# Loading w_in in row halves, two-half products for blocks 4 to 11, a cast of v on GpSimd and one more early product

## The chip, the cores and the metric

The kernel runs on one core of one Trainium2 chip. The core has a matrix engine (TensorE, PE in the profile; its weight loads are PEld), VectorE (DVE), ScalarE (ACT), GpSimd (POOL), a queue engine (SyncE, SP) and 16 DMA engines that all queues share. The metric is the device time of one execution in microseconds; of several runs the median is used.

## The reference, cut to what matters

Linear attention for 8 batches of 8 heads, 576 tokens and 64 columns, and on its output, as 4608 tokens of 512 columns, a two-layer network with a "snake" activation:

```
q_s = softmax of q over the 64 columns;  k_s = softmax of k over the 576 tokens
kv  = k_s^T v            (64 x 64 per batch and head)
x   = q_s kv             (4608 x 512, heads side by side)
h   = x @ w_in           (512 -> 2048)
g   = h + sin(alpha * h)^2 / alpha
out = g @ w_out          (2048 -> 512)
```

All inputs and the output are f32; the kernel computes its products in bf16 with f32 accumulation.

## The kernel before, in words

**Tiles.** The 4608 tokens make nine tiles of 512. For a tile, `mm_h` makes h in 16 blocks of 128 hidden columns: each block is four products (one per 128 rows of w_in, called chunks, taken in the order `KO` = 0, 2, 1, 3) of 128 x 128 weights on 512 tokens, accumulated in one PSUM bank. `sine` then runs the sine on ACT and the square on ACT, GpSimd or DVE (a letter string tells which: A, P, D), and `combine` adds h and the scaled square on DVE into `g`. `mm_o` and the generators `o_quad` and `o_stream` make the output from g and w_out.

**Order.** Everything is issued in the order in which the program is written (a manual schedule): each engine works through its own instructions in that order and waits on semaphores. Nothing is reordered.

**The start.** SP loads halves of batch 0's q, k and v. GpSimd waits for the first half of k (`held`, L355), then issues from its own queue the second half of v in two pieces (columns j 0 to 4, and 5 to 8) and all of w_in, converting f32 to bf16 on the way (`load_win`, L108): columns 0 to 255 and 256 to 511 of chunks 0 and 2; columns 0 to 511 of chunks 1 and 3; four transfers of 256 columns with all four chunks (columns 512 to 1535); columns 1536 to 2047; then the first half of w_out in two transfers (L111). All but the 512 KB ones of the last columns and of w_out carry 128 or 256 KB as they arrive in bf16. ACT makes the exponentials, DVE the sums and the normalization of q; two casts bring the second half of v to bf16 (`cast_v0`, L352), both on DVE. `wide_mm` makes kv, `attn_x` makes x, which goes to `xT` by ACT and DVE. x comes in two halves: chunks 0 and 2 of tile 0 first, chunks 1 and 3 later.

**Early products.** Between the first half of x and the second, three products of tile 0 are issued (block 0, chunks 0 and 2; block 1, chunk 0). After the products that make the second half of x, five more follow (block 1 chunk 2, blocks 2 and 3 with chunks 0 and 2). Then the main loop of tile 0 goes through the 16 blocks: blocks 0 to 3 get their chunks 1 and 3, blocks 4 to 15 all four in one go (`h_slot`, with `flush(lag, 1)`, so that the combine lags one block behind).

**Banks.** `BANKS[0]` gives tile 0's blocks their PSUM banks: blocks 0, 1 the two of kind a; 2, 3 b; 4 k (a single bank that also holds kv); 5, 6 l; 7, 8 a; 9, 10 b; 11 k; 12, 13 l; 14, 15 a. A bank is free for its next user when the combine of its block has read it: block 7 waits for block 0's, block 8 for 1's, 11 for 4's, 12 for 5's. The first four outputs of tile 0 take b, b, l, l, so the third waits for block 12's combine.

**What hangs on the loop.** After blocks 6 and 12 a tiny DVE copy (`load_q1`, L464) releases the SP queue to load batch 1: the first half of q behind the first copy, the second half of q and all of k and v behind the second. After blocks 8 and 10 GpSimd issues the next parts of w_out (rows of blocks 8 to 11, then 12 and 13), behind the squares that stand ahead on it. Batch 1's attention (L498 casts its v) runs between tile 0's output products; its x gives tile 1.

Of the kernel before, what the change touches and what calls it, by code (L numbers as in the profile page):

```python
# [23 lines left out]
def kernel(  # L24
# [82 lines left out]
    def load_win(c0, c1, cc=slice(0, 4)):  # L107
        nc.gpsimd.dma_start(out=win[:, cc, c0:c1], in_=win_v[:, cc, c0:c1])  # L108
# [159 lines left out]
    def bank(kind):  # L268

        if kind == "k":  # L270
            return ps_k.tile([128, 2, MF], F32, name="kvp", tag="a")[:, 0]
        pool = {"a": lambda: ps_h[0], "b": lambda: ps_h[1], "l": lambda: ps_l, "o": lambda: ps_o[0], "p": lambda: ps_o[1]}[kind]()
        return pool.tile([128, MF], F32, name={"l": "lp", "o": "op", "p": "op"}.get(kind, "hp"), tag=kind)

    def mm_h(t, ni, k0=0, k1=4):

        if ni == 0 and k0 == 0:
            G[t] = gpool.tile([128, nN, MF], BF16, name="g")
        hp = HP[t, ni] if k0 else bank(BANKS.get(t, 3 * "aabb" + "abba")[ni])
        HP[t, ni] = hp  # L280
        for k in range(k0, k1):
            nc.tensor.matmul(hp, win[:, KO[k], ni * 128:(ni + 1) * 128],  # L282
                             xT[:, KO[k], t * MF % NX:t * MF % NX + MF], start=(k == 0), stop=(k == 3))
        return hp

    def sine(t, ni, hp, sq):
        s = spool.tile([128, MF], F32, name="s")
        nc.scalar.activation(s, hp, AX.Sin, scale=alpha_sb[:, ni:ni + 1])  # L288
        if sq == "A":
            nc.scalar.activation(s, s, AX.Square)  # L290
        elif sq == "P":
            nc.gpsimd.tensor_tensor(s, s, s, op=ALU.mult)  # L292
        else:
            nc.vector.tensor_tensor(s, s, s, op=ALU.mult)
        return s
# [25 lines left out]
    ACT_CP, DVE_CP, GP_CP = nc.scalar.copy, nc.vector.tensor_copy, nc.gpsimd.tensor_copy  # L321
# [28 lines left out]
    def cast_v0(ii, j0, j1, eng):  # L350
        vv = vb[0].rearrange("p j (i c) -> p i j c", i=4)
        eng(vv[:, 2 * ii:2 * ii + 2, j0:j1, 0:D], staged["v", 0][:, ii::2, j0:j1])  # L352
# [5 lines left out]
    for c in range(2):  # L358
        load_win(256 * c, 256 * c + 256, slice(0, 4, 2))
    load_win(0, 512, slice(1, 4, 2))  # L360
    for c in range(2, 6):
        load_win(256 * c, 256 * c + 256)
    load_win(1536, 2048)
    for c in range(2):
        load_wout(4 * c, 4 * c + 4)
# [41 lines left out]
    tp1 = ps_l.tile([128, 8, 128], BF16, name="tp", tag="l")  # L407
    q_transpose_ii(0, 1, 0, 8, tp1)
    ACT_CP(alpha_sb, tpa)
    cast_v0(1, 0, 5, DVE_CP)  # L410
    cast_v0(1, 5, 9, DVE_CP)
    DVE_CP(A["qT", 0][:, 1, 0:8], tp1)

# [4 lines left out]
    wide_mm(0, 1)  # L418
    wide_norm(0, 1)
    nc.vector.reciprocal(inva_sb, alpha_sb)  # L420
    for ni, ki in ((0, 0), (1, 0), (0, 1)):
        mm_h(0, ni, ki, ki + 1)
    xp = [bank("l") for _ in range(2)]
    attn_x(0, 1, 0, 8, xp)
    for x in range(2):
        (ACT_CP, DVE_CP)[x](xT[:, 2 * x + 1, 0:MF], xp[x])
    nc.scalar.activation(zero, zero, AX.Sin)
    for ni, ki in ((1, 1), (2, 0), (2, 1), (3, 0), (3, 1)):
        mm_h(0, ni, ki, ki + 1)

    def h_slot(t, ni, sq, lag):
        hp = mm_h(t, ni, 2 if ni < (4, 2, 0)[min(t, 2)] else 0)
        lag.append((t, ni, hp, sine(t, ni, hp, sq)))

    def flush(lag, keep):
        while len(lag) > keep:
            combine(*lag.pop(0))
# [21 lines left out]
    with ES:  # L459
        def load_q1(ii):  # L460
            if ii == 0:
                staged["q", 1] = stage.tile([128, 4, J, D], F32, name="st_q", tag="st")
            st = staged["q", 1]
            DVE_CP(st[:, ii, 0, 0:1], zero)  # L464
            nc.sync.dma_start(out=st[:, ii::2, 0:8].rearrange("p i j d -> p i (j d)"),
                              in_=src_view(q, 1)[:, ii::2, 0:8 * D])

        def load_kv1():
            for n in "kv":
                staged[n, 1] = stage.tile([128, 4, J, D], F32, name=f"st_{n}", tag="st")  # L470
            for n, t, ii, j0, j1 in (("k", k, 0, 0, J), ("v", v, 0, 0, J), ("k", k, 1, 0, J),
                                     ("v", v, 1, 0, 5), ("v", v, 1, 5, J)):
                nc.sync.dma_start(out=staged[n, 1][:, ii::2, j0:j1].rearrange("p i j d -> p i (j d)"),
                                  in_=src_view(t, 1)[:, ii::2, j0 * D:j1 * D])

        late = {6: lambda: load_q1(0), 8: lambda: load_wout(8, 12), 10: lambda: load_wout(12, 14),
                12: lambda: (load_q1(1), load_kv1())}
        for ni in range(nN):
            h_slot(0, ni, "DPPAPPAPPAAPPAPD"[ni], lag)
            flush(lag, 1)  # L480
            if ni in late:
                late[ni]()
# [95 lines left out]
        for ni in range(nN):  # L578
            h_slot(1, ni, SQ[ni], lag)
            flush(lag, 1)  # L580
            if ni == 6:
                scale_q8()
            late_q8(ni)
# [69 lines left out]
    for ni in range(nN):  # L653
        h_slot(2, ni, SQ2[ni], lag)
        flush(lag, 2)
        if ni == 5:
            attn_kv(3)
        elif ni in (9, 13):
            ii = ni // 12
            x_copy(DVE_CP, slice(ii, 4, 2), 3, x_pair(3, ii))  # L660
    flush(lag, 0)

    for t in range(3, nT):
# [11 lines left out]
        for ni in range(nN):  # L675
            hp = mm_h(t, ni)
# [62 lines left out]
```

## Time and profile before

| what | value |
|---|---|
| time, median of 3 runs | 282.33 us (281.98 to 282.49) |
| profiled execution | 283.14 us, span in the profile 281.3 us |
| TensorE busy | 268.4 us, 95% |
| ACT / DVE / GpSimd busy | 224.2 / 187.1 / 80.2 us |
| granted TensorE clock | 0.999 |
| DMA | 46.06 MB, mean 164 GB/s |

The span is the time from the first to the last instruction in the profile of one execution; the execution's own time is a little longer. The timeline rows are: start in us, duration in us, engine, line, operation, output <- inputs, shape, number of merged instructions, and in brackets the idle time before with what ended it. In rows of stretches (start:end) the columns are the length, the busy time of PE, PEld, DVE, ACT and POOL with their counts, the granted clock, the DMA engines' share and GB/s.

### The profile page before, as it was taken

To read this page: it belongs to the slowest core of one execution; us is meant where nothing else is said; L and a number is where in the kernel's file an instruction comes from. 1 tells how busy PE (TensorE), PEld (TensorE's weight loads), DVE (VectorE), ACT (ScalarE), POOL (GpSimd) and SP (SyncE) were. 2 spreads that over 40 slices of the span, in tenths; PEclk is the share of its full clock that TensorE was granted. 3 is DMA by queue.
4 is the path that set the end of the run, shared out by engine and by line. 5 is a ranking of instruction groups with operands and counts; after the bars stand their busy time and mean duration, and the time that the engine had idled before them with its cause. 6 is when DMAs were issued, how large, how long until landed. Compare 5 with 4: busy or idle time off the path is not lost.

```text
span 281.3 us, 4775 instructions
## 1 busy us (share of the span) xinstructions
PE 268.4 (95%) x1814; PEld 124.2 (44%) x1843; DVE 187.1 (67%) x279; ACT 224.2 (80%) x321; POOL 80.2 (28%) x75
## 2 busy tenths in 40 slices
PE   3899999999999999999999999999999999999994
PEld 1434454444444444444444444444444444444443
DVE  2968867999878767766776677577775555555422
ACT  4799457999588999899989998999877777777400
POOL 2959112678667450215011500350000000000000
PEclk9999999999999999999999999999999999999999
DMA  7999999795699039811981199125011111111143
GB/s 258 299 185 224 276 385 401 266 356 198 156 245 379 3 76 294 336 37 43 328 332 37 40 267 384 37 51 123 10 30 37 37 40 37 38 42 44 41 100 75
DMA packets 39607, 46.06 MB, mean 164 GB/s; under 512 B 17040, under 2 KB 22944, under 8 KB 39584
## 3 DMA queue, kind: packets, MB, share of 16 engines
q1 hardware_dynamic: 33952, 41.11, 46.1%
q0 software_dynamic: 5472, 4.52, 9.8%
q8 instruction: 14, 0.23, 0.3%
q10 hardware_dynamic: 160, 0.13, 0.2%
q14 instruction: 9, 0.07, 0.1%
HBM read 36.71 MB, written 9.44 MB: 164 GB/s over the span
## 4 chain that ended last, share of the span: by engine, by line
PE 87%; DMA 8%; POOL 2%; issue 1%; ACT 0%; SPq 0%; DVE 0%
PE hp L282 38%; PE op L302 37%; DMA wout<-in_moe_w_out_dram 4%; PE hp L302 2%; DMA win<-in_moe_w_in_dram 2%; PE lp L282 2%; DMA st_k<-in_k_dram 2%; PE kvp L173 2%; PE lp L302 1%; PE op L282 1%; PE op L709 1%; PE hp L237 1%; POOL s L292 1%; PE xp L237 1%; PE kvp L282 1%
## 5 line engine op out<-in xcount | busy, mean ns | idle before, releaser
L298 DVE SCALAR_TENSOR_TENSOR g<-s,inva_sb,hp 128x512 bf16<-128x512 f32 x129 | 95.1, 745 | 58.9 <-ACT s L290 53.3
L282 PE MATMUL hp<-xT,win 128*128 128x512 bf16 x508 | 128.8, 379 | 0.8 <-DMA win<-in_moe_w_in_dram 0.4
L302 PE MATMUL op<-wout,g 128*128 128x512 bf16 x463 | 117.6, 379 | 1.7 <-issue 1.3
L288 ACT ACTIVATE s<-hp,alpha_sb 128x512 f32<-128x512 f32 x129 | 87.0, 684 | 21.8 <-PE hp L282 20.3
L282 PEld LDWEIGHTS <-win 128*128 128x128 bf16 x576 | 55.6, 98 | 68.4 <-DMA win<-in_moe_w_in_dram 1.8
L302 PEld LDWEIGHTS <-g 128*128 128x128 bf16 x560 | 53.4, 98 | 65.4 <-issue 2.9
L290 ACT ACTIVATE s<-s 128x512 f32<-128x512 f32 x112 | 70.7, 632 | 3.6
L292 POOL TENSOR_TENSOR s<-s 128x512 f32<-128x512 f32 x28 | 29.5, 1066 | 17.8 <-ACT s L288 17.7
L152 POOL TENSOR_TENSOR qn<-qe,qs 128x1152 bf16<-128x1152 bf16 x11 | 23.2, 2128 | 30.7 <-DVE qs L146 26.3
L314 DVE COPY o<-op 128x512 f32<-128x512 f32 (+2 forms) x32 | 21.1, 660 | 9.7 <-PE op L302 7.4
L137 POOL CAST vb<-st_v 128x1152 bf16<-128x1152 f32 x12 | 14.4, 1228 | 44.5 <-DMA st_v<-in_v_dram 44.2
L118 ACT ACTIVATE qe<-st_q 128x1152 bf16<-128x1152 f32 (+2 forms) x18 | 17.7, 1026 | 6.3 <-DMA st_q<-in_q_dram 6.1
L118 ACT ACTIVATE ke<-st_k 128x1152 bf16<-128x1152 f32 x16 | 17.9, 1153 | 2.6 <-DMA st_k<-in_k_dram 2.6
L145 DVE TENSOR_REDUCE qs<-qe 128x36 f32<-128x2304 bf16 x5 | 12.8, 2552 | 8.3 <-ACT qe L118 8.3
L302 PE MATMUL hp<-wout,g 128*128 128x512 bf16 x45 | 12.0, 379 | 0.5 <-DMA wout<-in_moe_w_out_dram 0.3
L118 ACT ACT_TABLE_LOAD x7 | 9.0, 1283 | 0.8 <-PEq L723 0.7
L302 PE MATMUL lp<-wout,g 128*128 128x512 bf16 x32 | 9.2, 379 | 0.1
L369 PE MATMUL warm<-st_q,ident 128*128 128x512 f32 (+1 forms) x6 | 4.1, 806 | 4.7 <-DMA st_q<-in_q_dram 4.7
L282 PE MATMUL lp<-xT,win 128*128 128x512 bf16 x32 | 7.7, 379 | 0.4 <-DMA win<-in_moe_w_in_dram 0.4
L250 DVE CAST xT<-xp 128x1024 bf16<-128x1024 f32 (+1 forms) x7 | 7.4, 1065 | 0.0
L298 DVE SCALAR_TENSOR_TENSOR g<-s,inva_sb,lp 128x512 bf16<-128x512 f32 x8 | 5.7, 739 | 0.4 <-POOL s L292 0.4
L108 POOL DMA_DIRECT2D win<-in_moe_w_in_dram x8 | 5.9, 772 | 0.0
(98 smaller groups left out, 137.2 us busy)
## 6 DMA issues: line engine op xcount, KB each, us to landing
out_dram<-o SPq DMA_DIRECT2D x70, 128.0 KB, 2.3
st_q<-in_q_dram SPq DMA_DIRECT2D x6, 1152.0 KB, 6.3
st_k<-in_k_dram SPq DMA_DIRECT2D x6, 1152.0 KB, 9.1
st_v<-in_v_dram SPq DMA_DIRECT2D x6, 1152.0 KB, 11.3
st_k<-in_k_dram SPq DMA_DIRECT2D x4, 576.0 KB, 8.3
st_q<-in_q_dram SPq DMA_DIRECT2D x4, 512.0 KB, 6.2
wout<-in_moe_w_out_dram POOLq DMA_DIRECT2D x3, 512.0 KB, 13.7
win<-in_moe_w_in_dram POOLq DMA_DIRECT2D x5, 256.0 KB, 7.9
```

The lines of the kernel that those rows point to most:

```text
L118: nc.scalar.activation(dst[:, :, ii * 128:(ii + 1) * 128].rearrange("p j (x d) -> p x j d", x=2), src[:, ii::2], AX.Exp)
L137: engs[ii](vv[:, 2 * ii:2 * ii + 2, :, 0:D], staged["v", b][:, ii::2])
L145: nc.vector.tensor_reduce(qs, A["qe", b].rearrange("p j (i d) -> p j i d", i=4), axis=AXL.X, op=ALU.add)
L152: engs[ii % len(engs)].tensor_tensor(qn[:, ii, 0:j1].rearrange("p j (x d) -> p j x d", x=2), qe[:, ii], part.unsqueeze(3).to_broadcast([12 ...
L250: eng(xT[:, c, d0:d0 + m - n], xp[..., n:m])
L282: nc.tensor.matmul(hp, win[:, KO[k], ni * 128:(ni + 1) * 128], xT[:, KO[k], t * MF % NX:t * MF % NX + MF], start=(k == 0), stop=(k == 3))
L288: nc.scalar.activation(s, hp, AX.Sin, scale=alpha_sb[:, ni:ni + 1])
L290: nc.scalar.activation(s, s, AX.Square)
L292: nc.gpsimd.tensor_tensor(s, s, s, op=ALU.mult)
L298: nc.vector.scalar_tensor_tensor(G[t][:, ni], in0=s, scalar=inva_sb[:, ni:ni + 1], in1=hp, op0=ALU.mult, op1=ALU.add)
L302: nc.tensor.matmul(acc, G[t][:, ni, j * 128:(j + 1) * 128], wout[:, ni, :], start=(ni == 0), stop=(ni == nN - 1))
L314: eng(o[:, cols], acc)
```

## The change

- Columns 512 to 1535 of w_in come in four transfers as before, but each has 512 columns and two chunks: columns 512 to 1023 with chunks 0 and 2, then with chunks 1 and 3; then columns 1024 to 1535 likewise.
- The first of the two casts of v's second half (j 0 to 4) moves from DVE to GpSimd, where it stands between the first and the second of these transfers.
- Four instead of three early products are issued ahead of the second half of x (block 1, chunk 2 in addition), and so four instead of five behind it.
- Blocks 4 to 11 of tile 0 are made in two halves: before block 4, the chunk 0 and 2 products of blocks 4, 5, 6 and 7; before block 8, those of 8 to 11; the loop then adds chunks 1 and 3, block by block.

One cast changes its engine; otherwise no instruction is added or taken away, and the number of DMAs and their bytes stay.

```diff
-    for c in range(2, 6):
-        load_win(256 * c, 256 * c + 256)
+    load_win(512, 1024, slice(0, 4, 2))
+    cast_v0(1, 0, 5, GP_CP)
+    load_win(512, 1024, slice(1, 4, 2))
+    for r in range(2):
+        load_win(1024, 1536, slice(r, 4, 2))
     load_win(1536, 2048)
...
     ACT_CP(alpha_sb, tpa)
-    cast_v0(1, 0, 5, DVE_CP)
     cast_v0(1, 5, 9, DVE_CP)
     DVE_CP(A["qT", 0][:, 1, 0:8], tp1)
...
-    for ni, ki in ((0, 0), (1, 0), (0, 1)):
+    for ni, ki in ((0, 0), (1, 0), (0, 1), (1, 1)):
         mm_h(0, ni, ki, ki + 1)
...
-    for ni, ki in ((1, 1), (2, 0), (2, 1), (3, 0), (3, 1)):
+    for ni, ki in ((2, 0), (2, 1), (3, 0), (3, 1)):
         mm_h(0, ni, ki, ki + 1)
...
-        hp = mm_h(t, ni, 2 if ni < (4, 2, 0)[min(t, 2)] else 0)
+        hp = mm_h(t, ni, 2 if ni < (12, 2, 0)[min(t, 2)] else 0)
...
         for ni in range(nN):
+            for n in range(ni, ni + 4) if ni in (4, 8) else ():
+                mm_h(0, n, 0, 2)
             h_slot(0, ni, "DPPAPPAPPAAPPAPD"[ni], lag)
```

## The prediction

> **What bounds the kernel now.** I read the page first (busy shares and slices), then the chain that ended last, then only the stretch that the edit touches: TensorE's timeline from 10 to 46 us with what ended its idle time, the ACT, DVE and GpSimd timelines beside it, the stretches with their DMA rates, and the queue's own waits.
>
> ```profile
> PE 268.4 (95%) x1814; PEld 124.2 (44%) x1843; DVE 187.1 (67%) x279; ACT 224.2 (80%) x321; POOL 80.2 (28%) x75
> DMA  7999999795699039811981199125011111111143
> ```
>
> TensorE is busy 95% of the span, and the 16 DMA engines are full in the first eight slices (to about 56 us). TensorE's instructions stay the same in number and kind, so the time can change only by TensorE's idle time. After 60 us it shows nothing but gaps of 0.16 us that no wait explains; what can be won or lost lies before 45 us.
>
> ```profile
> 12.83 0.82 PE L282 MATMUL hp<-xT,win 128*128 128x512 bf16 x2
> 13.62 0.41 PE L237 MATMUL lp<-qT,kvw 64*64 64x512 bf16 x4
> 15.57 1.90 PE L282 MATMUL hp<-xT,win 128*128 128x512 bf16 x8 [0.36 <-DMA win<-in_moe_w_in_dram]
> 17.31 1.03 PE L282 MATMUL kvp<-xT,win 128*128 128x512 bf16 x4
> 19.90 3.62 PE L282 MATMUL hp<-xT,win 128*128 128x512 bf16 x16
> 23.36 0.81 PE L282 MATMUL kvp<-xT,win 128*128 128x512 bf16 x3
> 24.55 1.90 PE L282 MATMUL lp<-xT,win 128*128 128x512 bf16 x8 [0.39 <-DMA win<-in_moe_w_in_dram]
> 29.74 1.89 PE L302 MATMUL lp<-wout,g 128*128 128x512 bf16 x8
> 35.39 0.38 PE L302 MATMUL hp<-wout,g 128*128 128x512 bf16 x1 [0.30 <-DMA wout<-in_moe_w_out_dram]
> ```
>
> These are tile 0's products. Sixteen take 3.46 us (19.90 to 23.36), so one starts every 0.216 us and ends 0.38 us after its start. There are three waits, each for a transfer: before 15.57 (the third w_in transfer), before 24.55 (columns 1536 to 2047) and before 35.39 (w_out 8 to 11). A gap is counted from the last product's end, so the issue time lost is different: the product after 23.36's four could start at 24.22, so 0.33 is lost there; 32 products after 28.02 end their issue at 34.93, so 0.46 is lost at the third.
>
> ```profile
> 9.20 6.33 DMA win<-in_moe_w_in_dram
> 24.54 10.81 DMA wout<-in_moe_w_out_dram
> 17.20:21.20 4.00, 4.00 (x21) 1.80 (x20) 3.48 (x6) 3.95 (x7) 3.22 (x4) 1.00 1.40 203
> 21.20:24.50 3.30, 2.96 (x14) 1.27 (x13) 2.86 (x5) 3.24 (x7) 2.81 (x3) 1.00 1.23 204
> ```
>
> The chain gives the landings: 15.53 and 35.35, after 6.3 and 10.8 us in the queue. The two stretches (last column GB/s) are the same queue with 256-column rows (17.2 to 21.2) and with 512-column rows (21.2 to 24.5): 203 and 204 GB/s.
>
> ```profile
> 16.28 2.42 ACT L288 ACTIVATE s<-hp,alpha_sb 128x512 f32<-128x512 f32 x4
> 19.27 0.67 ACT L288 ACTIVATE s<-kvp,alpha_sb 128x512 f32<-128x512 f32 x1
> 20.02 2.04 POOL L292 TENSOR_TENSOR s<-s 128x512 f32<-128x512 f32 x2 [0.35 <-ACT s L288]
> 21.10 0.75 DVE L298 SCALAR_TENSOR_TENSOR g<-s,inva_sb,kvp 128x512 bf16<-128x512 f32 x1
> 28.28 1.41 DVE L298 SCALAR_TENSOR_TENSOR g<-s,inva_sb,lp 128x512 bf16<-128x512 f32 x2 [0.19 <-POOL s L292]
> SPq L465 <- DVE st_q L464: 23.9, 2, 19.1
> ```
>
> ACT works without a break from 16.28 to 29.1, half a microsecond behind TensorE. Sine, square and combine of block 4 free bank k at 21.85; the combine of block 12 frees the first lp bank at 29.03, and its second user wants it at 29.74. The last line is the SP queue, which stands behind a tiny DVE copy before it may load batch 1.
>
> **The change part by part.** The sum is made on the profiled execution (span 281.3, 283.14 with what lies around it, 0.81 above the median of 282.33), and its difference is put on the median.
>
> *GpSimd's cast.* GpSimd's 640-element cast takes 0.73 us (at 41.77) where DVE took 0.48. The piece of v that it reads lands 4.8 us after its issue at 6.14, at 10.98; the fourth w_in issue is over at 10.65. So the cast runs from 11.0 to 11.75 and the six transfers queued behind it on GpSimd (three row halves of w_in, columns 1536 on, w_out twice) are issued 1.1 us later. What covers it: these landed 7.9 to 16.7 us after their issue, against 4.8 for the first ones, so they wait for DMA engines, not for GpSimd; and GpSimd stood idle 2.48 us before its first square at 17.63. Cover gone, it costs up to 1.1. DVE gains nothing: its other cast waits for the second piece (issued 7.04, 4.6 to land: 11.6). TensorE's kv product at 11.96 waited for ACT until 11.97; a cast ready by 11.8 leaves it there.
>
> *The early product.* Four early products instead of three end at 13.70, so the x product moves from 13.62 by 0.09; nothing is gained behind, as TensorE waits until 15.57 for the transfer anyway. ACT's sine at 16.28 waits for that product, 0.1 after its table was ready. Cost 0; 0.09 if the transfer came earlier.
>
> *The rows.* The same bytes with 512-column rows. From the two rates the gain over 1 MB is about 0.03 us; against it stands the third transfer, the only early one of this form: by issue plus time to landing it came 2.23 us behind its predecessor (13.30 to 15.53), while the fourth, same bytes in 256-column rows, took 1.71 (to 17.24) and the next 1.3 each. Bounds for the fourth: 17.1 to 17.76. I take 17.3, near the row of its own place in the queue; TensorE wants it at 17.30. The needs of the later ones are the same as before (19.03, 20.76, 22.5, 24.2), with over 0.5 us to spare except at the last.
>
> *The order of the products.* From 15.57: eight second halves to 17.30, eight first halves of blocks 4 to 7 to 19.03, their second halves to 20.76, then first halves of 8 to 11. Block 4 is now complete at 19.63 instead of 18.34. Its sine starts at 19.72 instead of 19.27, ends 20.40, GpSimd's square 21.52, the combine 22.31. Block 11's first half, the last of its eight, wants bank k at 22.06: a new wait of 0.30. It ends TensorE's w_in products 8 to 11 at 24.52, where the transfer of columns 1536 on lands at 24.50: the old wait of 0.33 is consumed. Net 0.
>
> ACT pays more. Block 8 is complete at 23.39 instead of 21.8, its sine starts at 23.48 instead of 22.38; ACT has had no idle to make up 1.1 us. So the combine of block 12 ends at 30.14 instead of 29.03, where TensorE wants the lp bank at 29.74: a second new wait, 0.45. TensorE comes to w_out 8 to 11 at 35.37, which landed at 35.35. Its issue on GpSimd is 0.75 later, but lay 10.8 us in the queue. The old wait of 0.46 is consumed. Net -0.02.
>
> *Sum:* +0.30 - 0.33 + 0.45 - 0.46 = -0.04; with some 0.1 for the fourth transfer's upper half, +0.1 rounded: **282.4**.
>
> *The shared port.* In the trace, a DVE square beside GpSimd's took 1.00 us (50.75) instead of 0.69, while a DVE cast of 512 that began under GpSimd's 640-cast took 0.43. The Trainium skill, SBUF — State Buffer, section Who interferes with whom, says that a DVE cast in a two-port mode and a GpSimd instruction lock each other out whole. By that DVE's second cast waits until 11.75 at most, or GpSimd's until DVE's kv normalization is over; the sum would be 0.1 to 0.3 higher. The trace bears it out for the square and not for the cast.
>
> **Rivals.**
>
> 1. *Batch 1's loads come late (slower).* The DVE copy at 27.94 that lets SP go on stands behind block 11's combine, now 1.1 later. If the seven loads shift with their issue, v's last piece lands at 43.5 instead of 42.40; the kv product at 42.77 wants its cast by 43.05, so +1.0: 283.3. It decides from 42.6 on. Against it: DMA engines are full to 42 us and these loads landed 9 to 12 us after issue.
> 2. *The fourth transfer is as slow as the third (slower, small).* Landing at 17.76 moves everything behind by 0.46, and the waits consumed above no longer cover: 282.8.
> 3. *The port collision*: GpSimd's square beside DVE's took 1.33 instead of 1.04; a cast stretched by the same 0.3 makes x 0.3 late, ACT's first sine 0.2, and block 7's first half, which has 0.07 to spare, waits for block 0's combine: 282.6.
> 4. *The edit does what its form suggests (faster).* Fewer, longer rows and pauses in GpSimd's issuing bring the third transfer to 15.1, when TensorE is ready (its products end issue at 15.13), and all after it; then 0.44 goes: 281.9. To pass 0.56 the new bank waits must fail to come as well.
>
> **How the numbers follow.** 0.2% is 0.56 us, about what runs from 281.98 to 282.49 can tell from no change. Forecast 0.50 (282.1 to 282.7), rival 1 0.16, rival 2 0.17 (a third of it over the bound), rival 3 0.05, rival 4 0.12 (two thirds of it over the bound, where the bank waits are absent too). Slower: 0.16, 0.06 of rival 2, and 0.06 from the forecast's own tail, as each 0.1 that ACT falls further back moves the lp wait by 0.1: 0.28. Faster 0.08, same 0.64. The range goes from rival 4 to rival 1.
>
> **What would show it.** Right: a TensorE wait near 22.1 for bank k, one near 29.7 for the lp bank, no wait (or under 0.1) near 24.5 and 35.4; ACT idle before the sines of blocks 4 and 8; the first wait still ends near 15.5; block 12's combine ends near 30.1. Wrong: a gap at 17.3, landings of batch 1's v after 42.6, the third transfer landing before 15.3, or w_out 8 to 11 much later than 35.4.

## The result and the profile after

The changed kernel takes 282.68 us (median of 19 runs, 282.38 to 283.78); the kernel before 282.33 us (19 runs, 281.7 to 282.91). The ratio is 1.0023 with a 95% interval of 1.0015 to 1.0031: slower by 0.4 to 0.9 us, while the medians lie 0.35 us apart. The forecast was 282.4 and "no change"; the time lies in the range, the sign of the small difference is clear, and the middle of the interval lies just over the 0.2% that I had called no change. One execution of the kernel before, in the first experiment below, took 292.22 us at a granted clock of 0.949 and enters no ratio.

The two profiled executions alone would say the opposite: 282.86 after (span 281.1), 283.14 before (span 281.3). That is the first thing to explain.

TensorE's timeline of the changed kernel (start, duration, engine, line, operation, shapes, count, and idle time before with what ended it):

```profile
13.45 0.41 PE L237 MATMUL lp<-qT,kvw 64*64 64x512 bf16 x4
15.46 1.90 PE L282 MATMUL hp<-xT,win 128*128 128x512 bf16 x8 [0.63 <-DMA win<-in_moe_w_in_dram]
20.22 1.89 PE L282 MATMUL hp<-xT,win 128*128 128x512 bf16 x8
22.20 0.59 PE L282 MATMUL kvp<-xT,win 128*128 128x512 bf16 x2
24.36 1.89 PE L282 MATMUL lp<-xT,win 128*128 128x512 bf16 x8
27.81 1.89 PE L302 MATMUL hp<-wout,g 128*128 128x512 bf16 x8
29.96 1.89 PE L302 MATMUL lp<-wout,g 128*128 128x512 bf16 x8 [0.26 <-DVE g L298]
35.14 0.59 PE L302 MATMUL hp<-wout,g 128*128 128x512 bf16 x2
```

Both forecast waits are there. With 0.216 us from product to product, the eight from 20.22 are issued by 21.95, and block 11's first half starts at 22.20: 0.25 lost on bank k. The eight from 27.81 are issued by 29.54, and the first product on the lp bank starts at 29.96: 0.42 lost. The waits for columns 1536 on (24.55 before) and for w_out (35.39 before) are gone. The first wait, for the third w_in transfer, is longer (0.63 instead of 0.36), as the work ahead of it is done sooner.

The ACT timeline, then DVE's, of the changed kernel:

```profile
18.62 0.63 ACT L290 ACTIVATE s<-s 128x512 f32<-128x512 f32 x1
19.56 0.69 ACT L288 ACTIVATE s<-kvp,alpha_sb 128x512 f32<-128x512 f32 x1 [0.31 <-PE kvp L282]
23.26 1.26 ACT L288 ACTIVATE s<-hp,alpha_sb 128x512 f32<-128x512 f32 x2 [0.62 <-PE hp L282]
```

```profile
21.40 0.75 DVE L298 SCALAR_TENSOR_TENSOR g<-s,inva_sb,kvp 128x512 bf16<-128x512 f32 x1 [0.40 <-POOL s L292]
29.16 1.41 DVE L298 SCALAR_TENSOR_TENSOR g<-s,inva_sb,lp 128x512 bf16<-128x512 f32 x2 [0.19 <-POOL s L292]
```

ACT, which had no idle time here before, now stands idle 0.31 before the sine of block 4 and 0.62 before that of block 8. It never makes that up. Block 4's combine ends at 22.15 instead of 21.85, block 12's at 29.91 instead of 29.03, and these two free the banks for which TensorE waits. The chain that ended last tells the same; these are its shares by engine in the changed kernel:

```profile
PE 90%; DMA 4%; POOL 3%; DVE 1%; ACT 1%; issue 0%; SPq 0%; ACTq 0%
```

DMA had 8% of it before. The path of the start now runs through sine, square and combine.

### The profile page after: what moved, and what is told of

It reads as the page before. It is cut to its first block, busy times and chain, and to the rows that moved or that the text cites. A ratio compares the mean times of both kernels' runs of the same rounds, so it can differ in the third digit from the quotient of the medians.

```text
span 281.1 us, 4804 instructions
## 1 busy us (share of the span) xinstructions
PE 271.7 (97%) x1843; PEld 124.9 (44%) x1843; DVE 186.7 (66%) x278; ACT 223.8 (80%) x321; POOL 81.5 (29%) x76
## 4 chain that ended last, share of the span: by engine, by line
PE 90%; DMA 4%; POOL 3%; DVE 1%; ACT 1%; issue 0%; SPq 0%; ACTq 0%
PE hp L282 38%; PE op L302 37%; PE hp L302 3%; PE lp L302 3%; DMA win<-in_moe_w_in_dram 2%; DMA st_k<-in_k_dram 2%; PE kvp L173 2%; PE lp L282 2%; POOL s L292 1%; PE op L282 1%; PE op L713 1%; PE hp L237 1%; PE kvp L282 1%; DVE g L298 1%; ACT s L288 1%; PE xp L237 1%
## 5 line engine op out<-in xcount | busy, mean ns | idle before, releaser
L302 PE MATMUL op<-wout,g 128*128 128x512 bf16 x480 | 120.4, 379 | 0.0
L302 PE MATMUL hp<-wout,g 128*128 128x512 bf16 x48 | 12.7, 380 | 0.0
L372 PE MATMUL warm<-st_q,ident 128*128 128x512 f32 (+1 forms) x6 | 4.7, 913 | 4.6 <-DMA st_q<-in_q_dram 4.6
```

The lines of the kernel that those rows point to most:

```text
L302: nc.tensor.matmul(acc, G[t][:, ni, j * 128:(j + 1) * 128], wout[:, ni, :], start=(ni == 0), stop=(ni == nN - 1))
```

## The experiments

**Theory T:** the cost is the two bank waits (0.25 and 0.42 us), and in most executions of the kernel before there are no late transfers of that size behind which they could disappear. **Rival R:** the transfers got slower, by the row halves or by being issued later behind the cast. **Rival S:** ACT is simply overloaded at the start, and any relief gains, whatever the order. All ratios are to the kernel before, timed beside the version at hand; the time given is the median.

### Parts of the change alone

The kernel before, unchanged, for the noise:

> The kernel before, unchanged, for a second profile and as a measure of the noise. All theories: ratio 1.000 (within 0.001). Theory T (the cost of the change is its two new bank waits, 0.09 to 0.3 at 22 us and 0.42 of issue time at 30 us, and they cost because the typical execution before has shorter transfer waits than the profiled one, whose 283.14 lies above all timed runs): the span comes out near 280.5 instead of 281.3, and the waits at 15.6, 24.6 and 35.4 us sum to clearly less than 1.15 us. Rival R (the transfers themselves got slower by row halves and the late issues behind the cast): the waits are as in the first profile and the span near 281.3.

Measured: 282.36 us, ratio 1.0006 (0.9997 to 1.0015). Its profile is of the execution of 292.22 us, so the span and the waits that I expected stay untested by this run; the second profile of this kernel is further down.

The cast and the fourth early product, without the two-half order:

```diff
-    for c in range(2, 6):
+    load_win(512, 768)
+    cast_v0(1, 0, 5, GP_CP)
+    for c in range(3, 6):
         load_win(256 * c, 256 * c + 256)
...
-    cast_v0(1, 0, 5, DVE_CP)
...
-    for ni, ki in ((0, 0), (1, 0), (0, 1)):
+    for ni, ki in ((0, 0), (1, 0), (0, 1), (1, 1)):
...
-    for ni, ki in ((1, 1), (2, 0), (2, 1), (3, 0), (3, 1)):
+    for ni, ki in ((2, 0), (2, 1), (3, 0), (3, 1)):
```

> The kernel before with two parts of the change alone: the cast on GpSimd (behind the first of the four 256-column transfers) and the fourth early product. T: no bank wait, ratio 1.000 (0.999 to 1.001). R: the later issues cost, ratio 1.001 to 1.003, with later landings of columns 512 to 1535 than 17.2, 18.5, 19.9, 21.2.

Measured: 281.76 us, ratio 0.9998 (0.9988 to 1.0009). Issuing behind the cast cost nothing that this interval shows: the four transfers landed at 15.9, 17.2, 18.5 and 19.9 us. The waits of TensorE that its trace marks between 12 and 41 us are one line:

```profile
PE hp L302 <- issue: 0.2, 1, 0.2
```

It names no transfer and no bank. A smaller bank wait is there all the same, against T's "no bank wait": the eight products from 26.76 are issued by 28.49, the first one on the lp bank starts at 28.70, and block 12's combine ended at 28.64 (27.89 and 0.75). TensorE's rows, then DVE's:

```profile
26.76 1.89 PE L302 MATMUL hp<-wout,g 128*128 128x512 bf16 x8
28.70 1.89 PE L302 MATMUL lp<-wout,g 128*128 128x512 bf16 x8
27.89 1.41 DVE L298 SCALAR_TENSOR_TENSOR g<-s,inva_sb,lp 128x512 bf16<-128x512 f32 x2 [0.19 <-POOL s L292]
```

So with transfers as early as these the old order, too, comes to the lp bank before it is free: 0.21 us, where the first profile had 0.7 to spare.

The two-half order alone, on the old transfers:

```diff
         for ni in range(nN):
+            for n in range(ni, ni + 4) if ni in (4, 8) else ():
+                mm_h(0, n, 0, 2)
...
-        hp = mm_h(t, ni, 2 if ni < (4, 2, 0)[min(t, 2)] else 0)
+        hp = mm_h(t, ni, 2 if ni < (12, 2, 0)[min(t, 2)] else 0)
```

> The kernel before with the two-half order of blocks 4 to 11 alone, on the old 256-column transfers. T: the bank waits come back, and blocks 6 and 7 want their columns 0.87 us earlier (18.2 against a landing of 18.5: 0.3 more): ratio 1.002 to 1.004, a TensorE wait for the lp bank near 30 us. R: 1.000.

Measured: 283.09 us, ratio 1.0035 (1.0021 to 1.0048). The whole cost of the change, or more, is in this part. Its profile has the lp wait (0.43 of issue time) and, too short for a mark, the one for bank k (0.25 at 22.84):

```profile
16.02 1.90 PE L282 MATMUL hp<-xT,win 128*128 128x512 bf16 x8 [0.80 <-DMA win<-in_moe_w_in_dram]
30.61 1.89 PE L302 MATMUL lp<-wout,g 128*128 128x512 bf16 x8 [0.27 <-DVE g L298]
```

Of the extra 0.3 for blocks 6 and 7 that I expected, 0.08 shows in this execution: its third transfer landed so late, at 15.97, that TensorE came to block 6 at 18.62, and the fifth landed at 18.65. R falls: old transfers, same cost.

### The two bank waits taken away, one by one

One square of tile 0 from ACT to DVE, so that ACT's later sines come sooner:

```diff
-            h_slot(0, ni, "DPPAPPAPPAAPPAPD"[ni], lag)
+            h_slot(0, ni, "DPPAPPAPPADPPAPD"[ni], lag)
```

> The changed kernel with one square (tile 0, block 10) on DVE instead of ACT, so that ACT's later sines come 0.55 earlier; nothing else. T: block 12's combine ends near 29.4 instead of 29.9, the lp wait (0.42 of issue time) goes, 0.3 to 0.4 us faster than the changed kernel: ratio to before 1.000 to 1.001. R: 1.002, as the transfers stay.

Measured: 282.05 us, ratio 1.0002 (0.9990 to 1.0014), 0.6 below the changed kernel's median. Block 12's combine ends at 29.02, and the lp wait is gone; the one for bank k stays, as it should (0.25 at 21.86). The same edit in the kernel before is the control:

> Control: the kernel before with the same square of block 10 moved from ACT to DVE. T: there is no lp wait to take away (block 12's combine had 0.7 to spare), ratio 1.000 (0.999 to 1.001). Rival S (relieving ACT is worth 0.3 us by itself, whatever the order): 0.999 or below.

Measured: 282.19 us, ratio 0.9993 (0.9980 to 1.0007). The interval holds T's 1.000 and S's 0.999 alike, so this control does not settle S by itself; the next run shows that the cost goes without any relief of ACT.

Block 11 in one go:

```diff
-            for n in range(ni, ni + 4) if ni in (4, 8) else ():
+            for n in range(ni, min(ni + 4, 11)) if ni in (4, 8) else ():
...
-        hp = mm_h(t, ni, 2 if ni < (12, 2, 0)[min(t, 2)] else 0)
+        hp = mm_h(t, ni, 2 if ni < (11, 2, 0)[min(t, 2)] else 0)
```

> The changed kernel, but block 11 in one go as before, so that its first half no longer asks for bank k before block 8 is finished. T: no wait near 22 us; block 8 is complete 0.6 to 0.7 earlier, ACT falls only 0.4 back instead of 1.1, block 12's combine ends near 29.3 and the lp wait shrinks to 0.1 or goes: 0.3 to 0.6 us faster than the changed kernel, ratio to before 0.999 to 1.001. R: 1.002.

Measured: 282.13 us, ratio 0.9998 (0.9983 to 1.0014). This is the one idle time of TensorE from 12 to 36 us that the timeline marks:

```profile
15.41 1.90 PE L282 MATMUL hp<-xT,win 128*128 128x512 bf16 x8 [0.55 <-DMA win<-in_moe_w_in_dram]
```

Block 8's sine starts at 22.55 instead of 23.26, block 12's combine ends at 29.27 instead of 29.91, and of the 0.67 us of bank waits 0.07 is left, before the lp bank. All transfers, the cast and the early product of the change are in this kernel, and it is as fast as before, within some 0.4 us to either side. So the transfers cost nothing that these runs show, and what cost was the place of block 11's first two products, which stand ahead of block 8's second half and wait for a bank that is three engines away.

Both repairs together, block 11 whole and block 10's square on DVE:

```diff
-            for n in range(ni, ni + 4) if ni in (4, 8) else ():
+            for n in range(ni, min(ni + 4, 11)) if ni in (4, 8) else ():
                 mm_h(0, n, 0, 2)
-            h_slot(0, ni, "DPPAPPAPPAAPPAPD"[ni], lag)
+            h_slot(0, ni, "DPPAPPAPPADPPAPD"[ni], lag)
```

> The changed kernel with both bank waits taken away: block 11 in one go and block 10's square on DVE. T: no bank wait is left, ratio to before 0.999 to 1.000, 0.3 to 0.6 us faster than the changed kernel, no faster than either repair alone by more than 0.2 us, as one alone nearly removes the waits. R: 1.002.

Measured: 281.99 us, ratio 0.9995 (0.9985 to 1.0005). No faster than one alone, as expected, and not faster than the kernel before. But T's "no bank wait is left" failed:

```profile
18.10 0.59 PE L282 MATMUL hp<-xT,win 128*128 128x512 bf16 x2 [0.29 <-DVE g L298]
```

Here the third transfer landed at 14.14, TensorE ran ahead, and block 7's first half found block 0's combine unfinished (it ended at 18.05): a third bank wait, 0.45 of issue time, which the two-half order brings when the transfer is early. The run with the square on DVE shows it too, a gap of 0.20 at 18.16; its third transfer landed at 14.15.

### The lp wait made larger

Block 11's square from GpSimd to ACT:

```diff
-            h_slot(0, ni, "DPPAPPAPPAAPPAPD"[ni], lag)
+            h_slot(0, ni, "DPPAPPAPPAAAPAPD"[ni], lag)
```

> The changed kernel with the lp wait made larger: block 11's square on ACT instead of GpSimd, so that ACT's sine of block 12 comes later. T: block 12's combine ends 0.25 to 0.5 later, the lp wait grows by as much, ratio to before 1.003 to 1.004. S and R: no step, as ACT has over 3 us of idle time behind tile 0: 1.002.

Measured: 282.92 us, ratio 1.0025 (1.0010 to 1.0040). The wait grew, by a little less than T's 0.25 to 0.5:

```profile
30.52 1.89 PE L302 MATMUL lp<-wout,g 128*128 128x512 bf16 x8 [0.49 <-DVE g L298]
```

It is 0.49 instead of 0.26. Against the time, 0.2 us more is less than these intervals resolve: T's 1.003 is inside, and so is 1.002. The control in the kernel before:

> Control: the same burden on ACT in the kernel before. T: the 0.7 that block 12's combine has to spare takes it up, ratio 1.000 to 1.001.

Measured: 282.17 us, ratio 1.0002 (0.9985 to 1.0020). TensorE's waits from 12 to 41 us in it are one line, for the third transfer:

```profile
PE hp L282 <- DMA win<-in_moe_w_in_dram: 0.4, 1, 0.4
```

Block 12's combine ended at 29.16 there, and TensorE came to the bank at 29.32. The same burden costs nothing that this interval shows where there is time to spare. The two burdened kernels lie 0.75 us apart in their medians (282.92 and 282.17), the two without the burden 0.35, but the intervals are too wide to call that a step.

### What the transfers do from run to run

A second profile of the kernel before:

> The kernel before, unchanged, once more for a profile. T: the third w_in transfer lands earlier than 15.53 and columns 1536 on before 24.2, so that the waits near 24.6 and 35.4 are absent or under half of the first profile's; span 280.0 to 280.7; ratio 1.000.

Measured: 282.22 us, ratio 1.0012 (0.9992 to 1.0033). My expectation of the profile failed: the third transfer was earlier (14.88), but the two later waits were larger than in the first profile.

```profile
PE hp L302 <- DMA wout<-in_moe_w_out_dram: 0.7, 1, 0.7
PE lp L282 <- DMA win<-in_moe_w_in_dram: 0.5, 1, 0.5
```

The time of just this execution was 283.53, while the 12 timed ones lie from 281.68 to 284.81, half of them at or below 282.01. So the profile is again of an execution longer than most of its kernel. These are the landings in all profiles but that of 292.22 us (issue plus time to landing, us; the time is that of the profiled execution):

| kernel | third w_in | columns 1536 on | w_out 8 to 11 | waits for the last two | time |
|---|---|---|---|---|---|
| before | 15.53 | 24.50 | 35.35 | both | 283.14 |
| before, second profile | 14.88 | 24.52 | 35.77 | both | 283.53 |
| before, cast and early product | 14.31 | 22.90 | 32.45 | none | 281.61 |
| before, third transfer in two (see below) | 14.53, 15.22 | 23.41 | 33.26 | none | 281.82 |
| before, block 11's square on ACT | 15.45 | 23.38 | 33.50 | none | 282.24 |
| before, block 10's square on DVE | 14.65 | 23.77 | 34.32 | under 0.3 | 282.28 |
| before, two-half order alone | 15.97 | 24.58 | 33.68 | none | 283.82 |
| changed | 15.42 | 24.00 | 33.37 | none | 282.86 |
| changed, block 11's square on ACT | 15.75 | 23.82 | 33.09 | none | 283.43 |
| changed, block 10's square on DVE | 14.15 | 23.52 | 33.22 | none | 282.10 |
| changed, block 11 whole | 15.36 | 23.66 | 33.35 | none | 282.23 |
| changed, both repairs | 14.14 | 23.25 | 33.04 | none | 281.84 |
| changed, both repairs, third in two (see below) | 13.47, 15.90 | 24.82 | 35.90 | both | 283.66 |

The same transfer lands more than 3 us apart. The first six rows have the old order, and there the time rises with the landing of w_out 8 to 11, without exception, by 1.9 us in all. The sharpest comparison is of three executions whose third transfers landed within 0.1 us and whose w_out landed within 0.15: the changed kernel took 282.86, with block 11 whole 282.23, the kernel before with block 11's square on ACT 282.24. The first has 0.67 us of bank waits, the second 0.07, the third none, and it is longer by 0.62 to 0.63.

The lowest times, where the transfers presumably cost least, say the same: 281.63 to 281.70 before in its four sets of runs, 282.38 for the changed kernel, 281.83 with both repairs. The 0.7 between the first two agrees with the sum of the two bank waits, though no profile shows which waits the lowest executions had. The 0.13 to 0.2 that the repaired kernel keeps would fit the third bank wait, less the 0.21 that the old order can lose at the lp bank; no run isolates it. What makes the queue early or late in an execution no run here shows.

### Two attempts at a faster kernel

The third transfer in two, in the kernel before and in the repaired one:

```diff
-    load_win(0, 512, slice(1, 4, 2))
+    for c in range(2):
+        load_win(256 * c, 256 * c + 256, slice(1, 4, 2))
```

> The kernel before with its third w_in transfer (columns 0 to 511, chunks 1 and 3) in two, so that blocks 0 and 1 wait for the first 128 KB alone. If that landing sets when tile 0 starts and with it the spread from run to run, the first wait shrinks: ratio 0.998 to 0.9995 and a smaller spread. If the landings behind take over, 1.000; if one more issue on GpSimd delays the rest, above 1.000.

Measured: 281.82 us, ratio 0.9993 (0.9983 to 1.0002). The direction is as hoped, the interval still holds 1.000, and the spread (281.60 to 282.48 in 11 runs) is narrow, but so few runs do not prove that.

> The changed kernel with both bank waits taken away and the third w_in transfer in two. If both hold: ratio 0.998 to 0.9995, below each of the two alone or equal to the better one.

Measured: 283.36 us, ratio 1.0033 (1.0015 to 1.0051): a clear miss. The halves of the third transfer landed at 13.47 and 15.90 and the later ones late, so that waits appear all along:

```profile
12.08 0.69 PE L184 MATMUL kvp<-vb,ke 64*128 64x130 bf16 x18 [0.35 <-POOL vb L352]
24.87 1.90 PE L282 MATMUL lp<-xT,win 128*128 128x512 bf16 x8 [0.40 <-DMA win<-in_moe_w_in_dram]
35.94 0.59 PE L302 MATMUL hp<-wout,g 128*128 128x512 bf16 x2 [0.54 <-DMA wout<-in_moe_w_out_dram]
```

The cast, one more issue back in GpSimd's queue, is now late for the kv product; whether the same edit shifted the queue into its late form, or this execution only met it, one profile cannot tell. No version was faster than the kernel before by a clear interval.

## Why the prediction was right or wrong

- *The order of the products: right in mechanism, and close in size.* Forecast 0.30 at 22.06 and 0.45 at 29.74; measured 0.25 at 21.95 and 0.42 at 29.54. Block 12's combine: 30.14 forecast, 29.91 measured. The chain behind it was ACT falling back without means to catch up, by a forecast 1.1 us: the sine of block 8 starts 0.88 later, block 12's combine ends 0.88 later.
- *"The old wait is consumed", twice: the step that failed.* The sum set the new waits against 0.33 and 0.46 of transfer waits. In the changed kernel's profile both are gone, but the bank waits did not cover them: the transfers themselves landed earlier (24.00 for 24.50, and 33.37 for 35.35), ahead of TensorE, which came to them at 24.36 and 35.14. Between the two profiled executions the sum even comes out, 0.25 + 0.42 - 0.33 - 0.46 = -0.12, with a first wait that ends 0.11 earlier, of the 0.28 by which the changed one is shorter. The error was to put that difference on the median. The old waits were real in the profiled execution, whose 283.14 lies above all 19 timed runs; I had noted its gap of 0.81 to the median and not asked whether the two waits, 0.79 together, were that gap. Where the transfers are early, as in four of the six profiles with the old order, the netting has nothing, or under 0.5, to net, and the new waits cost up to their full 0.67. By the ratio the change cost 0.65 us (0.42 to 0.88), near the full sum and well over the forecast 0.1. That 282.68 lies in the range is owed to a wide range, 281.9 to 283.3, and so in part to luck. What stays open: no profile of the unchanged kernel is of an execution near its median, so that its typical execution has early transfers is inferred from its variants and its times.
- *The cast: right that it costs nothing, wrong that DVE gains nothing.* It ran from 10.94 to 11.67 as forecast. DVE's remaining cast took 0.43 instead of 0.75, x came 0.17 earlier instead of 0.09 later (13.45 for 13.62, 0.1 of it as this whole execution started earlier), and all of it was lost in the wait for the third transfer, as forecast for the early product.
- *The rows: right that they cost nothing.* The fourth transfer landed at 17.06, just under the lower bound of 17.1, and TensorE came to it at 17.20. The 0.1 that I added for its upper bound was not needed. These are the stretches of the changed kernel that answer to 17.2 to 21.2 and 21.2 to 24.5 (last column GB/s):

```profile
17.10:21.40 4.30, 4.30 (x22) 2.06 (x21) 3.38 (x6) 3.96 (x7) 3.12 (x4) 1.00 1.19 188
21.40:24.00 2.60, 2.51 (x13) 1.05 (x12) 2.35 (x5) 1.94 (x4) 2.00 (x2) 1.00 1.23 202
```

  188 GB/s with the longer rows, 203 with the shorter ones before: no gain from the row length shows.
- *Rival 1, batch 1's loads late: refuted in its premise.* The DVE copy that releases SP ended at 28.97 instead of 28.09, late as the rival said (by 0.88, not 1.1), and v's last piece was issued 0.88 later. Yet it landed at 41.68, earlier than 42.40. In these two executions the landing did not follow the issue, which fits loads that wait for DMA engines.
- *Rival 2* did not come (17.06, not 17.76). *Rival 3, the port:* the collision that I priced did not come either; GpSimd's cast took 0.73 with DVE's starting under its end; the run with both repairs and the third transfer in two shows such a collision (last section). But block 7's wait for block 0's combine, which I had as a by-product of it with "0.07 to spare", came by another road: an early third transfer. *Rival 4:* early landings happen (14.14 to 14.88 in several profiles), but with both orders, so they explain the spread and not the difference.

## What to carry to other kernels

A change that reorders products on a full engine moves the finishing time of each accumulation, not only the order in which its inputs are needed: splitting four blocks into halves finished the first of them 1.2 us later (19.52 instead of 18.34), and the engine behind, which had no idle time, carried that delay to the next user of its banks. Before netting a new wait against an old one, ask whether the old one is there in the typical run: a profiled execution longer than all timed ones can show waits that the median does not have. Where run-to-run spread is larger than the effect, compare executions whose transfers landed alike, compare the lowest runs, and take the suspected wait away in both kernels.

## What the runs showed of the hardware that I had not expected

- The landing of one and the same transfer moves by more than 3 us between executions at a granted clock of 0.998 to 1.000: w_out 8 to 11 at 32.45 in one and 35.77 in another, issued at 24.15 and 24.20. In the six profiles with the old order the time rises with this landing.
- A DVE cast of 512 elements per partition took 0.75 us in the kernel before, beside GpSimd's issuing of w_in transfers (the second of two casts in 1.15 us from 11.29), and 0.43 in the changed kernel, where it began under the end of GpSimd's own cast. That it ran beside the issuing does not explain this alone: the cast of 640 just before it ran beside it too and took 0.485, and most of the 0.43 ran beside the next issue, from 11.62. The two rows are of the changed kernel, from the timelines of GpSimd and of DVE:

```profile
10.94 0.73 POOL L352 CAST vb<-st_v 128x640 bf16<-128x640 f32 x1 [0.37 <-DMA st_v<-in_v_dram]
11.52 0.43 DVE L352 CAST vb<-st_v 128x512 bf16<-128x512 f32 x1 [0.28 <-DMA st_v<-in_v_dram]
```

  The Trainium skill, SBUF — State Buffer, section Who interferes with whom, has a DVE copy or cast in a two-port mode and GpSimd block each other for a whole instruction. The 0.32 between the two casts could be a block by GpSimd's issuing. The second pair overlaps by only 0.15, at the recorded end of GpSimd's cast, and DVE's took its undisturbed 0.43. In the run with both repairs and the third transfer in two, the same two casts overlap by 0.51, and both are longer:

```profile
11.23 0.80 POOL L352 CAST vb<-st_v 128x640 bf16<-128x640 f32 x1
11.52 0.80 DVE L352 CAST vb<-st_v 128x512 bf16<-128x512 f32 x1 [0.26 <-DMA st_v<-in_v_dram]
```

  That pair fits the rule: DVE's cast took 0.37 more, and GpSimd's next instruction begins 0.38 after DVE's start, at 11.90. So the prediction's reading that the trace does not bear the rule out for the cast rested on too short an overlap, 0.08 there (42.42 to 42.50). The square that the prediction counts for the rule is no cast. No run here isolates the port.
